# Recurrence, router and two feed-forward stages on one core: a written-out order with longer transfers and spare time for loads, and a first block inverted in two halves of 64 rows

## The chip, the cores and the metric

One NeuronCore of a Trainium2 chip. The time is device microseconds (us) of one execution. Engines: PE (TensorE; PEld its weight loads), DVE (VectorE), ACT (ScalarE), POOL (GpSimd), SP (SyncE, which issues nearly all DMAs). A run of the kernel before took 1150.17 us (median of 3).

## What is computed

```python
for t in range(S):                                # S = 768, 4 x 8 heads of 40
    y[:, :, t] = einsum('bhd,bhde->bhe', rt, state)
    Sa = einsum('bhde,bhe->bhd', state, at)
    state = state * wt - einsum('bhd,bhe->bhde', Sa, bt) + einsum('bhd,bhe->bhde', vt, kt)
# y as x[3072, 320] -> one of 8 experts each (argmax, softmax weight)
h = maximum(einsum('ecd,edf->ecf', disp, w1), 0); y = einsum('ecf,efd->ecd', h, w2)
# out = gate * y -> a dense pair of layers
h = x @ w_in; out = maximum(0.01 * h, h) @ w_out
```

## The kernel before

**The recurrence** (`attention`) does the 768 times in chunks of 32. A block `i` (6 of them) is four chunks for each of two groups of eight chunks; in the code a pair `n = 2i + hf` (hf 0 or 1), and within it four column groups `g`, which the loads and `prep` take two at a time (`h = 0` for g 0 and 1, `h = 1` for g 2 and 3). A **step** `s` is one (block, g, hf), `s = 8i + 2g + hf`: 48 steps, and step `s + 2` needs the state of step `s`.

For each block, ahead of its steps:
- `load` (L349 on, issued through `dma`, L343): decay `w`, keys `KB`, `AE`, from DRAM to SBUF, by SP;
- `prep` (L371 to L381): scans and products on DVE, some of them on POOL;
- `gram` (L397 on): 8 matmuls (L409; the profile counts each twice), a copy to `mab` by ACT, the store `Md<-mab`, and four masked copies into `AE` on DVE (L424);
- `inverse` (L438 on): `Mu<-Md` brings the block's 128 small triangular matrices back, one to a partition; POOL makes the start value `Tt` (L441, L442), DVE does 28 dependent operations (L450, L452), ACT or DVE copies the corner `Ta`, and SP stores `Td<-Tt` and `Tad<-Ta`;
- `back` (L456 on): `TB<-Td` (for each half `gp`) and four `Rt<-Tad` load them in the layout of the matmuls;
- `fix` (L465 on): matmuls L476 and L485 finish the inverse, for each `hf` and half `gp`.

Steps with g 0 and 1 use the half `gp` 0, the others `gp` 1. A step is `kbt` (L512), then `chain`: X (L542), u (L553, which is the first to need `fix`), state (L570, scaled into `MV` by DVE L574); then `output`: L590, L603, masks on DVE (L611), `py` (L622). After the four g of a pair the router (`Router.add`, L824 to L870) chooses experts and scatters the rows to DRAM. Then come the experts (L981, L1046) and the dense pair (L981, L1186), which the change does not touch.

**The order** is worked out while the program is built. `Sched.op` records each operation with its planned duration, what it reads and writes, and a due time; `Sched.run` places them one by one on V, A, P, T, S (DVE, ACT, POOL, PE, SP) by `level`, a due time less what still follows. `START` and `STEP` give the steps their due times, `DPREP`, `DINV`, `DFIX`, `DTURN`, `DOUT` those of the work around them, `RV0`, `ZR0` the earliest planned times of some DMAs. A transfer is planned as `nb / 360e3` us on one bus and seen .95 us after. Where the plan shows PE idle for over 0.24 us, `emit` puts filler matmuls ahead of the late operation (L724, `py<-one`, bf16 128 x 128, no use made of them) so that PE is not idle there. The engines then run in that order, each one in order, and wait on semaphores.

Of the kernel before, what the change touches and what calls it, by code (L numbers as in the profile page):

```python
# [10 lines left out]
ALU = mybir.AluOpType  # L11
# [15 lines left out]
class Sched:  # L27
# [7 lines left out]
    def __init__(self, eng):  # L35
        self.eng = dict(zip('VAPTS', eng))
        self.ops = []
        self.due = 1e9
        self.since = 0.
        self.slack = 0.  # L40
        self.w, self.r = {}, {}

    def op(self, on, dur, fn, r=(), w=(), ring=None, done=0., grp=None, xfer=0., banks=(), sel=False, act=None):
# [17 lines left out]
        self.ops.append(dict(on=on, fn=fn, deps=deps, ring=ring, done=done, grp=grp, users=0, ps=None, xfer=xfer, banks=list(banks), due=self.due, since=self.since, slack=self.slack, sel=sel, act=act))  # L61
        return i
# [20 lines left out]
    def run(self):  # L83
        ops = self.ops
        n = len(ops)
        succ = [[] for _ in ops]
        for i, o in enumerate(ops):
            for d in o['deps']:
                succ[d].append(i)
        lag = lambda o, e: self.AFTER[e] + o['done'] + (o['xfer'] + 1.5 if o['xfer'] else 0.)  # L90
        level = [0.] * n
        for i in range(n - 1, -1, -1):
            o = ops[i]
            e, d = min(o['on'].items(), key=lambda x: x[1])
            level[i] = d + max([level[j] + lag(o, e) for j in succ[i]] + [-o['due']])
        left = [len(o['deps']) for o in ops]
# [23 lines left out]
        while placed < n:  # L120
# [153 lines left out]
def attention(ctx, tc, I, R, eng):  # L274
# [62 lines left out]
    def masks(E):  # L337
# [4 lines left out]
        P.iota(maskZ.bitcast(I32)[:, D:D + 1], [[0, 1]], base=NT, channel_multiplier=0)  # L342
    def dma(o, i, nb, r, w, on='S'):  # L343
        op(on, .48 if on == 'S' else .06, lambda E: E.dma_start(o, i), r, w, xfer=max(.18, nb / 360e3))  # L344

# [3 lines left out]
    def load(n, h):  # L349
        i, hf = divmod(n, 2)  # L350
        a = n % 4
        late = ['Mu'] if n in (2, 3) else []
        dma(ws[hf][:, h, 0:528], I['wT'][hf, i, :, 528 * h:528 * h + 528], 270336, late if LATEW else (), [('w', hf, h)])
        dma(KBs[a][:, 2 * h:2 * h + 2].rearrange("x g p a t -> x (g p a t)"), I['kbT'][hf, i, :, 1024 * h:1024 * h + 1024], 1 << 19, late, [('KB', a, h)])
        src = I['aT'][hf, i].rearrange("x (j g c) -> x j g c", j=2, g=4)[:, :, 2 * h:2 * h + 2]
        zero = [('AEs', a, j, g, par) for j in range(2) for g in (2 * h, 2 * h + 1) for par in range(2)]
        if i:
            dma(AEs[a][:, :, 2 * h:2 * h + 2].rearrange("x j g p t -> x j (g p t)"), src.rearrange("x j g c -> x j (g c)"), 1 << 19, late, [('AEo', a, j, h) for j in range(2)] + zero)
# [78 lines left out]

    def inverse(i):  # L438

        dma(Mu, Mds[i % 2].rearrange("c u t s -> (c u) t s"), 1 << 19, [('Md', i % 2, c, par) for c in range(8) for par in range(2)], ['Mu'])  # L440
        op('P', 1.47, lambda E: (E.affine_select(Tt, Mu, [[-1, 32], [1, 32]], ALU.is_gt, 0.0, base=0, channel_multiplier=0),  # L441
                                 E.memset(Ttf[:, 0:1024:33], -1.0)), ['Mu'], ['Tt'])  # L442
        for k in range(1, 15):
            m = 15 - k
            if i:
                when(8 * i - 8 + DINV[0] + (DINV[1] - DINV[0]) * k / 14)
            tv = tmp[:, 0:2 * k * m].rearrange("u (x a b) -> u x a b", x=2, b=m)
            tt = Tb[:, :, 0:k, k + 1:16]
# [3 lines left out]
            op('V', d, lambda E, tv=tv, tt=tt: E.tensor_tensor(tt, tt, tv, ALU.subtract), ['tmp'], ['Tt'])  # L452
        op(ev(256, 'AV'), 0, lambda E: copy(E, Ta, Tt[:, 0:16, 0:16].rearrange("u a b -> u b a")), ['Tt'], ['Ta'])
        dma(Tds[i % 2].rearrange("u q s t -> (u q) s t"), Tt, 1 << 19, ['Tt'], [('Td', i % 2)], QI)
        dma(Tads[i % 2].rearrange("u q s t -> (u q) s t"), Ta, 1 << 17, ['Ta'], [('Tad', i % 2)], QI)

    def back(i):

        for gp in range(2):
            dma(TB4s[i % 2][:, gp].rearrange("s h u t -> s (h u) t"), Tds[i % 2][16 * gp:16 * gp + 16].rearrange("u q s t -> (q s) u t"), 262144,  # L460
                [('Td', i % 2)], [('TB', 4 * (i % 2) + 2 * gp + h) for h in range(2)], QI)
# [120 lines left out]
    def output(s):  # L582
# [41 lines left out]
        if g == 3:  # L624
            xk = []
            for bb in range(2):
# [3 lines left out]
                while u < 8 * bb + 8:  # L630
# [47 lines left out]
    for m, t in enumerate(NIs):  # L678
        for j in range(2):
            r = RHO[j]  # L680
            op(ev(320), 0, lambda E, t=t, r=r, j=j: copy(E, t[r:r + 64, j, :, :], ident[r:r + 64, r:r + 40].unsqueeze(1).broadcast_to([64, 8, 40])), (), [('NI', m, j, par) for par in range(2)])
    when(0)
    inverse(0)
    back(0)
    for x in range(4):
        when(2 * (x // 2) + x % 2)
        fix(0, x % 2, x // 2)
    Q.slack = 0.
    for i in range(6):
        if i < 5:  # L690
            for h in range(2):
                for n in (2 * i + 2, 2 * i + 3):
                    when(8 * i + DPREP[2 * h + n % 2])
                    load(n, h)
                    prep(n, h)
# [5 lines left out]
            for x in range(4):  # L701
                when(8 * i + DFIX + .5 + x // 2 * 1.5)
                fix(i + 1, x % 2, x // 2)
            when(8 * i + DTURN)
            turn(2 * i + 2)
            turn(2 * i + 3)
        for c in range(8):
# [8 lines left out]
            if i == 0 and c < 4:  # L716
# [710 lines left out]
```

## Time and profile before

| | us (or a count) |
|---|---|
| runs | 1150.17 (1149.91 to 1153.44), 3 runs |
| profiled execution: its time, its span | 1148.05, 1146.3 |
| step 0 (L553) to the last `py` of step 47 | 85.15 to about 543 |
| experts and dense pair, from 543 on | 603.3 |
| busy in the span | PE 1009.7, DVE 735.6, ACT 552.8, POOL 378.5 |
| PE's matmuls and weight loads; packets of the instruction queue q8 | 15,918 and 15,918; 127 |

The page gives totals; the kernel has stages, so a stretch is read at a time. Busy of PE is the union of its matmuls; "issue" as a releaser is time in which PE waited for nothing that the profile shows. A row of a timeline is start, duration, engine, line, operation, tiles, shapes and count.

### The profile page before, as it was taken

The page shows a single profiled execution, that of the slowest core. Times are in us where ns is not written, and L with a number is a line of the kernel's source. Part 1 is how long each engine was busy: PE and PEld are TensorE (multiplying, and loading weights), DVE is VectorE, ACT ScalarE, POOL GpSimd, SP SyncE. Part 2 cuts the span into 40 slices and gives each one's busy share as a digit, 9 for nine tenths or more (in the row PEclk, how much of TensorE's full clock was granted, in tenths as well). Part 3 has the DMA queues.
Part 4 walks back from the last instruction along what each step waited for, and adds up shares of the span by engine and source line. Part 5 has one row for each costly group of instructions (what it writes and reads, how often), then busy time and mean ns, then how long its engine had stood idle before and what let it go on. Part 6 is the DMA issues. An engine that isn't in the chain of part 4 may idle for free.

```text
span 1146.3 us, 37065 instructions
## 1 busy us (share of the span) xinstructions
PE 1009.7 (88%) x15918; PEld 906.1 (79%) x15918; DVE 735.6 (64%) x1571; ACT 552.8 (48%) x1264; POOL 378.5 (33%) x318
## 2 busy tenths in 40 slices
PE   4677777888878879989589999999999999999997
PEld 4665667777767767778588888999989999999997
DVE  7984676976967856344577787786764444444453
ACT  4114554856746747667434434434533333333343
POOL 8232112222223221010155565662849191010100
PEclk9876888998989988889799999999999999999999
DMA  7659463653734723330565666753311010000000
GB/s 201 202 135 250 100 164 90 178 150 110 194 98 146 172 64 98 72 98 12 165 224 175 199 197 199 217 170 107 99 32 51 18 30 18 7 18 7 23 13 14
DMA packets 146123, 129.44 MB, mean 113 GB/s; under 512 B 102176, under 2 KB 110624, under 8 KB 145952
## 3 DMA queue, kind: packets, MB, share of 16 engines
q1 hardware_dynamic: 143648, 119.11, 37.7%
q0 software_dynamic: 2304, 7.89, 1.9%
q8 instruction: 127, 2.08, 0.8%
q14 instruction: 44, 0.36, 0.1%
HBM read 102.13 MB, written 24.85 MB: 111 GB/s over the span
## 4 chain that ended last, share of the span: by engine, by line
PE 56%; DVE 14%; issue 13%; ACT 6%; DMA 5%; POOL 3%; SPq 3%; POOLq 0%; DVEq 0%; ACTq 0%
PE ph L981 17%; PE py L622 4%; PE oy L1188 3%; PE oy L1187 3%; PE oy L1186 3%; PE ch L570 2%; PE tr L590 2%; SPq L344 2%; PE tr L409 2%; ACT Z L292 2%; PE tr L512 2%; DVE tmp L450 2%; ACT NI L292 2%; PE y L1046 2%; PE tr L485 2%
## 5 line engine op out<-in xcount | busy, mean ns | idle before, releaser
L981 PE MATMUL ph<-xt,wq 128*128 128x512 f32 (+2 forms) x1408 | 311.5, 364 | 5.0 <-DVE xt L1022 5.0
L981 PEld LDWEIGHTS ph<-xt,wq 128*128 128x128 f32 x1408 | 248.0, 189 | 35.5 <-DVE xt L1022 6.5
L1166 DVE TENSOR_TENSOR gf<-gf,ph 128x512 f32<-128x512 f32 (+1 forms) x112 | 68.4, 610 | 98.8 <-ACT gf L1165 98.4
L1170 DVE TENSOR_TENSOR gl<-gf,gh 128x512 fp32r<-128x512 f32 (+1 forms) x112 | 76.7, 684 | 70.1 <-ACT gh L1169 70.1
L1165 ACT ACTIVATE gf<-ph 128x512 f32<-128x512 f32 (+1 forms) x112 | 60.0, 536 | 109.5 <-PE ph L981 109.0
L292 ACT COPY Z<-tr 40x512 f32<-40x512 f32 x192 | 98.3, 540 | 22.9 <-PE tr L590 21.2
L1169 ACT CAST gh<-gf 128x512 fp32r<-128x512 f32 (+1 forms) x112 | 62.7, 559 | 96.3 <-DVE gf L1166 96.3
L381 POOL TENSOR_TENSOR KB<-KB,w 128x1024 f32<-128x1024 f32 x21 | 47.2, 2245 | 159.4 <-PE py L622 34.4
L1196 POOL DMA_INDIRECT out_dram<-ob,gid x24 | 23.9, 995 | 218.5 <-ACT ob L1195 213.3
L1032 ACT ACTIVATE gh<-ph 128x448 fp32r<-128x448 f32 x64 | 34.9, 546 | 120.3 <-PE ph L981 120.3
L1188 PE MATMUL oy<-wo,gl 128*128 128x320 f32 x288 | 89.2, 310 | 0.1
L1187 PE MATMUL oy<-wo,gh 128*128 128x320 f32 x288 | 88.9, 309 | 0.0
L1186 PE MATMUL oy<-wo,gh 128*128 128x320 f32 x288 | 88.8, 308 | 0.0
L622 PE MATMUL py<-Z,RE 128*32 128x40 f32 x1536 | 73.7, 212 | 6.1 <-DVE RE L611 4.6
L611 DVE TENSOR_TENSOR RE<-tr,maskP 64x128 f32<-64x128 f32 x192 | 55.1, 287 | 34.3 <-PE tr L603 30.4
L622 PEld LDWEIGHTS py<-Z,RE 128*32 128x32 f32 x1536 | 65.8, 120 | 13.6 <-DVE RE L611 7.5
L1046 PE MATMUL y<-gh,wo 128*128 128x448 f32 x192 | 73.1, 381 | 3.0 <-DVE Y L1053 2.8
L574 DVE TENSOR_TENSOR MV<-ch,WC 40x320 f32<-40x320 f32 x92 | 44.9, 488 | 45.3 <-PE ch L570 43.7
L870 POOL DMA_INDIRECT xs<-xb,rii x24 | 25.6, 1068 | 142.0 <-DVE rii L860 95.2
L1049 PE MATMUL y<-gl,wo 128*128 128x448 f32 x192 | 70.9, 369 | 0.0
L292 ACT COPY NI<-tr 64x160 f32<-64x160 f32 x192 | 55.1, 287 | 23.3 <-PE tr L512 20.0
L590 PE MATMUL tr<-ident,MV 128*104 128x128 f32 x384 | 60.2, 290 | 5.1 <-ACT NI L292 4.1
(173 smaller groups left out, 2206.2 us busy)
## 6 DMA issues: line engine op xcount, KB each, us to landing
KB<-in_kbT_dram SPq DMA_DIRECT2D x24, 512.0 KB, 6.0
RE<-in_rT_dram SPq DMA_DIRECT2D x48, 256.0 KB, 4.3
AE<-in_aT_dram SPq DMA_DIRECT2D x20, 512.0 KB, 6.3
raw<-in_wo_dram SPq DMA_DIRECT2D x16, 640.0 KB, 5.2
raw<-in_wqa_dram SPq DMA_DIRECT2D x16, 512.0 KB, 4.1
w<-in_wT_dram SPq DMA_DIRECT2D x24, 264.0 KB, 4.6
xs<-maskZ SPq DMA_DIRECT2D x8, 563.5 KB, 5.5
win<-xs SPq DMA_DIRECT2D x8, 563.5 KB, 10.0
```

The costliest lines, as they stand in the source:

```text
L292: (E.copy if E is A else E.tensor_copy)(o, i)
L590: E.transpose(c['t'][0:104, q, :], MV[:, 4 * h + q], ident)
L622: E.matmul(py[32 * g:32 * g + 32, b, col:col + 40], RE[:, j, p, :], Z[:, p, ZC[j]:ZC[j] + 40], start=True, stop=True)
L981: T.matmul(ph, l, r, start=k == 0, stop=k == 7)
L1046: T.matmul(y[c], hi, gh, start=m == 0, stop=False)
L1049: T.matmul(y[c], hi, gl, start=False, stop=m == 7)
L1166: V.tensor_tensor(gf, gf, ph, ALU.max)
L1169: A.copy(gh, gf)
L1170: V.tensor_tensor(gl, gf, gh.bitcast(F32), ALU.subtract)
L1186: T.matmul(o, gh[:, sl], w[:, 0:320], start=m == 0, stop=False)
L1187: T.matmul(o, gh[:, sl], w[:, 320:640], start=False, stop=False)
L1188: T.matmul(o, gl[:, sl], w[:, 0:320], start=False, stop=m == 15)
```

## The change

The planner's transfers get longer: `nb / 230e3` us instead of `nb / 360e3`, seen 2.0 us after instead of .95. What needs a load is planned `SPARE` 5.11 + `LATE` 0.737 us after that (for the first reader; writers of a load's buffer add `SPARE` in `level`); operations of `fix` and of the router get .296 us, those of `output` .065 us more. The first block's inverse is recorded for `h` 0 and `h` 1 apart: `inverse(0, (h,))` works on 64 partitions, `back` and `fix` on one half, each behind that half's grams. Due times and earliest times have other values. The arithmetic is the same.

```diff
-        lag = lambda o, e: self.AFTER[e] + o['done'] + (o['xfer'] + 1.5 if o['xfer'] else 0.)
+        lag = lambda o, e: self.AFTER[e] + o['done'] + (o['xfer'] + 2.2 if o['xfer'] else 0.)
...
-            level[i] = d + max([level[j] + lag(o, e) for j in succ[i]] + [-o['due']])
+            level[i] = d + max([level[j] + lag(o, e) + ops[j]['spare'] for j in succ[i]] + [-o['due']])
...
-                seen = bus + .95
+                seen = bus + 2.
...
-                at[j] = max(at[j], seen)
+                at[j] = max(at[j], seen + ops[j]['spare'] + (self.LATE if o['free'] else 0.))
...
+    SPARE, LATE = 5.11, 0.737
-    SLACK, PATIENCE, ALPHA = 0.075, 30.677, 0.105
+    SLACK, PATIENCE, ALPHA = 0.075, 61.165, 0.105
...
-SLACK0, LD0, LDS, PR0, PRS, LATEW, RV0, ZR0, ZRS, GR = 0.268, 0.0, 3.0, 15.245, 0, 0, 40.584, 52.618, 7.65, 1
+SLACK0, LD0, LDS, PR0, PRS, LATEW, RV0, ZR0, ZRS, GR = 0.353, 0.0, 3.0, 14.965, 0.69, 0, 59.595, 76.525, 7.65, 1
...
-START, STEP = 66.553, 7.916
-DPREP, DINV, DOUT, DTURN, DFIX = (-1.52, -1.13, -0.18, 1.52), (2.13, 2.32), 1.968, 0.886, 6.599
+IN0, IN1, LD1 = -11.529, 31.742, 28.586
+LEAD, SPO, SPF = 0.74, 0.065, 0.296
+START, STEP = 42.156, 7.328
+DPREP, DINV, DOUT, DTURN, DFIX = (-2.42, -2.48, -0.18, 1.93), (2.35, 3.65), 1.966, 0.961, 7.992
...
-        op(on, .48 if on == 'S' else .06, lambda E: E.dma_start(o, i), r, w, xfer=max(.18, nb / 360e3))
+        op(on, .48 if on == 'S' else .06, lambda E: E.dma_start(o, i), r, w, xfer=max(.18, nb / 230e3), free=free)
...
-    def inverse(i):
+    def inverse(i, parts=(0, 1)):
...
+        o, n = 64 * parts[0], 64 * len(parts)
+        H, C = slice(o, o + n), range(4 * parts[0], 4 * parts[-1] + 4)
...
+        dma(Mu[H], Mds[i % 2][C[0]:C[-1] + 1].rearrange("c u t s -> (c u) t s"), 4096 * n, [('Md', i % 2, c, par) for c in C for par in range(2)], kM)
...
             for g in (2 * h, 2 * h + 1):
                 gram(n, g)
+        Q.due = IN0 + IN1 * h
+        inverse(0, (h,))
+        back(0, (h,))
+        for hf in range(2):
+            fix(0, hf, h)
...
-    when(0)
-    inverse(0)
-    back(0)
-    for x in range(4):
-        when(2 * (x // 2) + x % 2)
-        fix(0, x % 2, x // 2)
```

Line numbers of the changed kernel are higher: 344 became 349, 409 414, 424 429, 441 451, 450 460, 452 462, 476 487, 485 496, 553 564, 570 581, 724 743.

How it moves the instructions, at three places. **SP, from the first block's `Mu<-Md` on**, before:

```order
L344 DMA Mu<-Md_182 128x1024
L344 DMA KB_134<-in_kbT_dram 128x1024
L344 DMA AE_130<-in_aT_dram 128x2x512
L344 DMA KB_135<-in_kbT_dram 128x1024
L344 DMA AE_131<-in_aT_dram 128x2x512
```

and the changed kernel, from the second half's `Mu<-Md`:

```order
L349 DMA Mu<-Md_182 64x1024
L349 DMA Td_184<-Tt 64x1024
L349 DMA Tad_186<-Ta 64x256
L349 DMA TB_145<-Td_184 128x16x32
L349 DMA Rt<-Tad_186 16x16x16 x4
L349 DMA KB_135<-in_kbT_dram 128x1024
L349 DMA KB_134<-in_kbT_dram 128x1024
L349 DMA AE_131<-in_aT_dram 128x2x512
L349 DMA AE_130<-in_aT_dram 128x2x512
L349 DMA KB_134<-in_kbT_dram 128x1024
L349 DMA Td_184<-Tt 64x1024
```

The eight loads of block 1 (tiles 130, 131, 134, 135) stood between `Mu` and `Td`; now they stand behind the first half's stores and loads, and three of the eight behind the second half's stores.

**DVE, where the first block's inverse begins**, before:

```order
L424 TENSOR_TENSOR AE_129<-ch,maskP 32x4x32 x4
L371 SCALAR_TENSOR_TENSOR W<-w_126,d_178 128x528
L375 SCALAR_TENSOR_TENSOR w_126<-w_126,d_178 128x528
L372 COPY WC_155<-W 128x16
L373 RECIPROCAL rC_157<-WC_155 128x16
L374 TENSOR_TENSOR Q_166<-W,rC_157 128x2x8x32
L371 SCALAR_TENSOR_TENSOR W<-w_127,d_178 128x528
L450 TENSOR_TENSOR tmp<-Mu,Tt 128x28
```

and the changed kernel:

```order
L429 TENSOR_TENSOR AE_129<-ch,maskP 32x4x32 x4
L429 TENSOR_TENSOR AE_128<-tr,maskP 32x4x32 x4
L429 TENSOR_TENSOR AE_128<-ch,maskP 32x4x32 x4
L460 TENSOR_TENSOR tmp<-Mu,Tt 64x28
L462 TENSOR_TENSOR Tt<-Tt,tmp 64x2x14
L460 TENSOR_TENSOR tmp<-Mu,Tt 64x52
```

The six operations for block 1 and two of the eight groups of masks are no longer ahead of it, and its 28 operations follow each other with nothing between; the second half's 28 come eight instructions after.

**PE, around step 0** (L553 before, L564 now), before:

```order
L553 MATMUL ch<-X_163,TB_145 32x40 x16
L391 MATMUL tr<-ident,Q_167 128x128 x4
L485 MATMUL tr<-TB_145,Wm_174 32x16 x32
L570 MATMUL ch<-MV_117,NI_143 40x40 x16
L409 MATMUL tr<-AE_131,KB_135 64x64 x16
L553 MATMUL ch<-X_164,TB_145 32x40 x16
```

and the changed kernel:

```order
L564 MATMUL ch<-X_163,TB_145 32x40 x16
L553 MATMUL ch<-MV_118,AE_129 32x40 x16
L523 MATMUL tr<-ident,KB_133 128x128 x4
L581 MATMUL ch<-MV_117,NI_143 40x40 x16
L414 MATMUL tr<-AE_131,KB_135 64x64 x16
L414 MATMUL tr<-AE_130,KB_134 64x64 x8
L564 MATMUL ch<-X_164,TB_145 32x40 x16
```

Of block 1's eight grams (8 matmuls each) six stood ahead of step 0 and two ahead of step 1; now none, three ahead of step 1, and all eight ahead of step 2. Fillers: 715 in all before, 1,065 now; 445 of them stood ahead of step 0, now 325.

## Rows read from the trace of the kernel before

**Rows 1.** Stretches: length, busy (count) of PE, PEld, DVE, ACT, POOL, clock, DMA.
```profile
85.15:170.56 85.41, 62.75 (x1877) 53.38 (x1869) 52.37 (x126) 41.76 (x118) 13.16 (x8) 0.78 0.69 175
170.56:250.23 79.67, 66.55 (x2071) 58.24 (x2069) 63.00 (x175) 50.86 (x143) 24.26 (x19) 0.90 0.56 146
```
**Rows 2.** What PE waited for, 85 to 543: sum, times, longest.
```profile
PE tr L485 <- issue: 11.4, 8, 2.3
...
PE py L622 <- DVE RE L611: 4.6, 8, 1.1
...
PE py L724 <- issue: 0.3, 1, 0.3
```
**Rows 3.** PE's order in time, around one pause.
```profile
113.97 0.43 PE L553 MATMUL ch<-X,TB 32*32 32x40 f32 x27
119.98 0.34 PE L553 MATMUL ch<-X,TB 32*32 32x40 f32 x3 [5.57 <-issue]
```
**Rows 4.** DMA, 85 to 543: instruction queue (packets, MB), then KB each and us to landing.
```profile
q8 instruction: 94, 1.54, 1.4%
...
Mu<-Md SPq DMA_DIRECT2D x5, 512.0 KB, 4.8
Td<-Tt SPq DMA_DIRECT2D x5, 512.0 KB, 3.2
TB<-Td SPq DMA_DIRECT2D x10, 256.0 KB, 4.4
Md<-mab SPq DMA_DIRECT2D x70, 32.0 KB, 3.2
```
**Rows 5.** DVE in order of time.
```profile
41.99 1.18 DVE L424 TENSOR_TENSOR AE<-ch,maskP 32x128 f32<-32x128 f32 x4
...
49.04 0.15 DVE L450 TENSOR_TENSOR tmp<-Mu,Tt 128x28 f32<-128x28 f32 x1
...
67.10 0.21 DVE L452 TENSOR_TENSOR Tt<-Tt,tmp 128x28 f32<-128x28 f32 x1
...
94.95 1.18 DVE L424 TENSOR_TENSOR AE<-tr,maskP 32x128 f32<-32x128 f32 x4
```
**Rows 6.** SP and POOL in order of time.
```profile
23.83 2.32 SPq L344 DMA_DIRECT2D Md<-mab  x4
...
42.53 0.43 SPq L344 DMA_DIRECT2D KB<-in_kbT_dram  x1
...
46.46 1.56 POOL L441 TENSOR_SCALAR_AFFINE_SELECT Tt<-Mu 128x1024 f32<-128x1024 f32 x1 [13.35 <-DMA Mu<-Md]
```
**Rows 7.** A group of DVE: total busy, mean ns of one, idle before.
```profile
L452 DVE TENSOR_TENSOR Tt<-Tt,tmp 128x28 f32<-128x28 f32 (+6 forms) x84 | 21.3, 254 | 2.0
```
**Rows 8.** PE in order of time, up to step 8.
```profile
44.78 6.25 PE L724 MATMUL py<-one 128*128 128x128 bf16 x109
...
66.69 1.98 PE L409 MATMUL tr<-AE,KB 128*64 128x64 f32 x32 [3.95 <-DVE tmp L450]
...
75.10 1.06 PE L391 MATMUL tr<-ident,Q 128*128 128x128 f32 x8 [2.19 <-DVE Q L374]
...
81.92 0.68 PE L476 MATMUL tr<-Rt,TB 16*32 16x16 f32 x58 [0.18 <-DMA Rt<-Tad]
...
85.15 0.58 PE L553 MATMUL ch<-X,TB 32*32 32x40 f32 x19
...
99.73 0.47 PE L553 MATMUL ch<-X,TB 32*32 32x40 f32 x30
...
106.88 1.30 PE L570 MATMUL ch<-MV,NI 128*40 128x40 f32 x32
...
130.58 0.81 PE L570 MATMUL ch<-MV,NI 128*40 128x40 f32 x32
...
170.56 0.76 PE L553 MATMUL ch<-X,TB 32*32 32x40 f32 x32
```

More of the change, by code (lines that the diff above doesn't have):

```diff
@@ L40, in __init__, with op @@
         self.slack = 0.
+        self.spare = 0.
         self.w, self.r = {}, {}
-    def op(self, on, dur, fn, r=(), w=(), ring=None, done=0., grp=None, xfer=0., banks=(), sel=False, act=None):
+    def op(self, on, dur, fn, r=(), w=(), ring=None, done=0., grp=None, xfer=0., banks=(), sel=False, act=None, free=False):
         i = len(self.ops)
@@ L60, in op @@
         on = on if isinstance(on, dict) else {on: dur}
-        self.ops.append(dict(on=on, fn=fn, deps=deps, ring=ring, done=done, grp=grp, users=0, ps=None, xfer=xfer, banks=list(banks), due=self.due, since=self.since, slack=self.slack, sel=sel, act=act))
+        self.ops.append(dict(on=on, fn=fn, deps=deps, ring=ring, done=done, grp=grp, users=0, ps=None, xfer=xfer, banks=list(banks), due=self.due, since=self.since, slack=self.slack, sel=sel, act=act, free=free, spare=self.spare if on.keys() != {'S'} else self.SPARE if xfer and free else 0.))
         return i
@@ L357, in load @@
         if i:
-            dma(AEs[a][:, :, 2 * h:2 * h + 2].rearrange("x j g p t -> x j (g p t)"), src.rearrange("x j g c -> x j (g c)"), 1 << 19, late, [('AEo', a, j, h) for j in range(2)] + zero)
+            dma(AEs[a][:, :, 2 * h:2 * h + 2].rearrange("x j g p t -> x j (g p t)"), src.rearrange("x j g c -> x j (g c)"), 1 << 19, late, [('AEo', a, j, h) for j in range(2)] + zero, free=True)
         else:
@@ L436, in when @@
         Q.due = START + STEP * s
-    def inverse(i):
-        dma(Mu, Mds[i % 2].rearrange("c u t s -> (c u) t s"), 1 << 19, [('Md', i % 2, c, par) for c in range(8) for par in range(2)], ['Mu'])
-        op('P', 1.47, lambda E: (E.affine_select(Tt, Mu, [[-1, 32], [1, 32]], ALU.is_gt, 0.0, base=0, channel_multiplier=0),
-                                 E.memset(Ttf[:, 0:1024:33], -1.0)), ['Mu'], ['Tt'])
+    def inverse(i, parts=(0, 1)):
+        o, n = 64 * parts[0], 64 * len(parts)
+        H, C = slice(o, o + n), range(4 * parts[0], 4 * parts[-1] + 4)
+        kM, kT, kt = [[(x, h) for h in parts] for x in ('Mu', 'Tt', 'tmp')]
+        U = slice(o // 4, (o + n) // 4)
+        dma(Mu[H], Mds[i % 2][C[0]:C[-1] + 1].rearrange("c u t s -> (c u) t s"), 4096 * n, [('Md', i % 2, c, par) for c in C for par in range(2)], kM)
+        op('P', 1.47, lambda E: (E.affine_select(Tt[H], Mu[H], [[-1, 32], [1, 32]], ALU.is_gt, 0.0, base=0, channel_multiplier=0),
+                                 E.memset(Ttf[H, 0:1024:33], -1.0)), kM, kT)
         for k in range(1, 15):
@@ L452, in inverse @@
[L452 to L461, printed above, removed]
+            op('V', d, lambda E, tv=tv, k=k, m=m: E.tensor_tensor(tv, Mb[H, :, k:k + 1, k + 1:16].broadcast_to([n, 2, k, m]), Tb[H, :, 0:k, k:k + 1].broadcast_to([n, 2, k, m]), ALU.mult),
+               kM + kT, kt)
@@ new lines, in inverse @@
+            op('V', d, lambda E, tv=tv, tt=tt: E.tensor_tensor(tt, tt, tv, ALU.subtract), kt, kT)
+        op(ev(256, 'AV'), 0, lambda E: copy(E, Ta[H], Tt[H, 0:16, 0:16].rearrange("u a b -> u b a")), kT, [('Ta', h) for h in parts])
+        dma(Tds[i % 2][U].rearrange("u q s t -> (u q) s t"), Tt[H], 4096 * n, kT, [('Td', i % 2, h) for h in parts], QI)
+        dma(Tads[i % 2][U].rearrange("u q s t -> (u q) s t"), Ta[H], 1024 * n, [('Ta', h) for h in parts], [('Tad', i % 2, h) for h in parts], QI)
@@ L462, in back @@
+    def back(i, parts=(0, 1)):
+        for gp in parts:
+            dma(TB4s[i % 2][:, gp].rearrange("s h u t -> s (h u) t"), Tds[i % 2][16 * gp:16 * gp + 16].rearrange("u q s t -> (q s) u t"), 400000,
+                [('Td', i % 2, gp)], [('TB', 4 * (i % 2) + 2 * gp + h) for h in range(2)], QI)
+        g, e = parts[0], parts[-1] + 1
         for q in range(4):
-            dma(R4[32 * q:32 * q + 16].rearrange("s m u t -> s (m u) t"), Tads[i % 2][:, q].rearrange("u s t -> s u t"), 80000, [('Tad', i % 2)], [('Rt', m, q) for m in range(4)], QI)
+            dma(R4[32 * q:32 * q + 16, 2 * g:2 * e].rearrange("s m u t -> s (m u) t"), Tads[i % 2][16 * g:16 * e, q].rearrange("u s t -> s u t"), 80000, [('Tad', i % 2, h) for h in parts], [('Rt', m, q) for m in range(2 * g, 2 * e)], QI)
@@ L636, in output @@
                     u += m
+            Q.spare = SPF
             R.add(Q, psum, copy, ev, hf, i, xk)
+            Q.spare = SPO
     Q.slack = SLACK0
@@ L692, in attention @@
                 for n in (2 * i + 2, 2 * i + 3):
+                    when(8 * i + DPREP[2 * h + n % 2] - LEAD)
+                    Q.since = 0. if i else LD1
+                    load(n, h)
+                    Q.since = 0.
                     when(8 * i + DPREP[2 * h + n % 2])
-                    load(n, h)
                     prep(n, h)
@@ L721, in attention @@
             when(s + DOUT)
+            Q.spare = SPO
             output(s)
+            Q.spare = 0.
     Q.run()
```

20 lines of the change are left out of this document (10 added, 10 removed).

## The prediction

> **What bounds the kernel now.** The stretches come first. From step 8 on a block takes some 80 us, of which PE is busy 66.55 of 79.67; the first block's stretch takes 85.41 with 62.75 busy and a granted clock of 0.78, against 0.90 after [rows 1]. So PE is near its limit once the recurrence runs, and in the first block it has both the lower clock and more idle time. Next, what PE waited for from 85 us to 543: the ten groups "issue" sum to 57.9 us, and the largest named wait is only 4.6 [rows 2]. The timeline shows what such a pause is: 27 of 32 matmuls of one group run, then nothing for 5.57 us, then the rest [rows 3]. The same stretch has 94 packets on the instruction queue, 1.54 MB [rows 4]: a pause inside one group fits instructions that come late. What the change retimes, the waits for loads, is therefore not what PE loses most by after step 8. The start is another matter. The reader should see in the timelines that PE fills 6.25 us with 109 fillers at 44.78 [rows 8], while DVE does the inverse from 49.04 to 67.31 [rows 5] and SP then stores and reloads it; `fix` runs at 81.92 and step 0 at 85.15 [rows 8]. This chain bounds the first 85 us.
>
> **The change, part by part.**
>
> *Step 0 comes sooner.* The first half needs only the first four grams. Before, their four stores were issued until 26.15 [rows 6]; landing takes 3.2, then `Mu` 4.8 for 512 KB [rows 4] (taken whole: half as many bytes may be faster), with some 1 us of issue between: 35.1. POOL needs 1.56 [rows 6]: 37. DVE could begin the inverse at 49.04 less the 5.9 us between the masks' end (43.17) and there, less two of eight mask groups, 2.4 (two rows like 1.18): 40.7 [rows 5]. I take 39, between the two. 28 operations of 0.254 [rows 7] and small gaps, none interleaved, take 7.5, to 46.5; before they took 18.3. Half as many partitions is taken as no shorter; the bounds are 4 and 7.5. `Td` 3.2 and `TB` 4.4 [rows 4], with about 1.5 of issue: 55.6. From the last `fix` start to step 0 took 3.2 [rows 8]: step 0 at 58.5 to 59, **26.5 us sooner**. If each hop takes its longer bound and DVE the 40.7, it is 22; if half the bytes and rows are faster, 30.
> The rows give a landing of 3.2 us for as little as 32 KB and 4.8 for 512 KB [rows 4]. The Trainium skill ("DMA: Bandwidth & Descriptors", Anatomy of one DMA) fits a fixed 2.0 us and bytes over 436 GB/s, for a DMA issued another way. By it three hops of 256 KB would take 2.6 each (an estimate from that page), and step 0 would come some 4 us earlier still; the rows stand against it, and nothing below uses it.
>
> *Work moves behind step 0.* Six of block 1's grams stood ahead of step 0 and stand after it: three rows of 32 matmuls like 1.98, 5.6 in all, and two L391 groups, one row of 1.06 [rows 8]. **+6.7 us** on PE.
>
> *Fillers.* 350 more in all, but 120 fewer ahead of step 0, where PE is idle anyway; so 470 more after it. One takes 6.25 / 109 = 0.057 us [rows 8]: 26.8 us of PE. They stand where the plan sees a wait, and the plan now puts 5.11 + 0.74 us behind every load's landing. Where PE would have waited anyway, a filler costs nothing; where the load has long landed, its whole time. Bounds 0 and 26.8. The named waits are so small [rows 2] that most of the padding behind loads can't be real, but in the first block, now begun with less other work in hand, the order has the state's own chain to wait for, which is. I take half: **+13.4**.
>
> *Clock.* PE at 0.78 is at 1.2 GHz some 0.44 of the time. The same 32 matmuls take 1.30 there and 0.81 at 2.4 [rows 8]. If fillers lift the first block halfway to the 0.90 of the next [rows 1], 0.12 less of 62.75 us runs slow, and (1 - 0.81 / 1.30) of that is won: **-2.8**. Bounds 0 and -10.4 (none and all of the 0.44).
>
> *Costs beside other work.* 28 more DVE operations (7.1 us), 1.7 more on POOL, seven more DMA issues on SP (about 0.45 each). DVE has 33 us idle in the first block's stretch [rows 1], and the second half's inverse runs while step 0 waits for its transfers: nothing, and at most 7.1 if block 1's preparation, which DVE does next, is what PE waits for. The eight loads of block 1 were issued from 42.53 [rows 6]; now they are behind the first half's `Rt`, about 51.5. That is 9 us later, and block 1's grams on PE are behind them. I cost it at nothing as long as fillers and steps 0 and 1 cover it; the second rival is what happens if not.
> The span's 31,836 matmuls and weight loads came in 127 packets (the table), 251 each, so 700 more are 2.8 packets. The pauses come to 57.9 / 94 = 0.62 us a packet [rows 2, 4]: some 1.7 us, which I leave within the rounding. The Trainium skill ("Runtime: NRT & Kernel Launch", Instruction fetch mechanics) says that the fetch of the next block of instructions is mostly hidden; by it the sum would lose this term, and the 5.57 us pause speaks against it.
>
> Sum: -26.5 + 6.7 + 13.4 - 2.8 = **-9.2 us** on the profiled execution's 1148.05: 1138.9. Experts and dense pair are the same instructions. The median of the runs is 2.1 above the profiled one; with it, 1141. I say **1140**.
>
> **The rivals.**
>
> *The whole start is kept*: nearly all new fillers stand in real waits and the clock rises. Then, with 1 us left of the fillers and the clock nearer its bound, -26.5 + 6.7 + 1 - 8 = -27: 1122. For it: the first block's low clock. Against it: small named waits.
>
> *The start's gain ends at step 2.* All eight grams of block 1 now stand ahead of step 2's u on PE. They need the loads, 9 us later than before, and DVE's preparation. Before, its last masks ended at 96.1 and step 2 ran at 99.73 [rows 5, 8]. From 43.17 to 96.1 DVE spent 18.3 on the inverse, so 34.7 on the rest; begun again behind the second half's inverse, at about 57, it ends at 92. Then step 2 gains 6 or 7 only, and of the fillers some 370 come after it: half of them, +10.6, and the clock, -2.8, leave +1: 1149 to 1151. No change. It decides if PE stands before block 1's grams with its fillers done.
>
> *Slower: the fillers are simply work.* PE has little slack after step 8, and a filler that covers no wait delays every step behind it. With none covered and the clock as before: -26.5 + 6.7 + 26.8 = +7: 1157. It decides if fewer than (26.8 + 6.7 - 26.5) / 26.8, about a quarter, of the new fillers stand in waits. For it: the 240 fillers from step 8 on become 430, where PE waited least. Against: the plan of before left the waits of the first block without fillers.
>
> *The change does nothing*, because the halves are serialised again: the second half's `Mu` stands ahead of the first half's `Td` on SP, so the first half's stores wait for the second half's grams. Their masks ended at 43.17 before [rows 5], ahead of the 46.5 at which `Td` is ready, so I give it no chance of its own.
>
> **How the numbers follow.** Forecast 0.50, of which a little ends near no change; whole start kept 0.14; ends at step 2 0.16; slower 0.20. Less than 0.3%, about 3.4 us, can't be told from no change. Faster: 0.46 + 0.14 = 0.60; same 0.04 + 0.14 = 0.18; slower 0.20 + 0.02 = 0.22. The likeliest case's own range is 1127 to 1149. The range for 8 in 10 takes in most of the two outer cases: 1119 to 1156, leaving out the half of the first below its 1122 and those of the slower that are worse than 1156 because loads come late too.
>
> **What would show it.** Step 0's u at 57 to 63 us and the first half's inverse begun near 39, in under 8 us: the start is right. Step 2's u at 99.73 less 7 or more, and step 8's below 165, would show it kept; step 2 at 92 to 98 and step 8 at 168 to 172, the second rival. Whether the fillers cover waits shows in the blocks from step 8 on: at 79.67 or less they do, at 82 or more they don't. A clock above 0.84 in the first block shows that term. I am wrong at the root if step 0 isn't at least 15 us sooner, or if blocks after step 8 lose or win more than 4 us each, which the views of before give no reason for.

## The result and the profile after

The changed kernel takes **1162.22 us** (median of 4 runs, 1161.25 to 1169.63), the kernel before beside it 1150.53 (1149.91 to 1153.44): ratio 1.0118, 95% interval 1.0078 to 1.0158. It is 1.2% slower; the forecast was 1140, and 1162 lies outside its range of 1119 to 1156. The profiled execution has a span of 1161.3 (before 1146.3).

Three stretches divide the difference: up to step 8's u, from there to the first matmul of the experts, and the rest. The first fence is the view by stretches of the kernel before (length, busy of PE with its matmuls, PEld and the other engines, granted clock, DMA), for the first two, then the same for the fillers alone (L724); the second fence is the changed kernel (fillers L743).

```profile
0.00:170.56 170.56, 115.44 (x2820) 102.34 (x2820) 126.28 (x269) 64.77 (x172) 56.51 (x80) 0.83 0.66 176
170.56:558.51 387.95, 322.78 (x9931) 280.66 (x9930) 255.68 (x787) 249.74 (x693) 83.62 (x77) 0.89 0.44 114
...
0.00:170.56 170.56, 32.68 (x475) 30.48 (x475) 0.83 0.66 176
170.56:558.51 387.95, 22.20 (x240) 16.33 (x240) 0.89 0.44 114
```

```profile
0.00:169.55 169.55, 126.53 (x3004) 113.99 (x3004) 136.07 (x306) 74.02 (x195) 57.86 (x84) 0.86 0.64 167
169.55:573.40 403.85, 337.69 (x10097) 292.93 (x10096) 255.42 (x769) 243.86 (x678) 86.81 (x77) 0.87 0.43 114
...
0.00:169.55 169.55, 44.60 (x635) 40.85 (x635) 0.86 0.64 167
169.55:573.40 403.85, 35.36 (x430) 27.56 (x430) 0.87 0.43 114
```

Taking the fillers from PE's busy time leaves its own work, and taking all of it from the length leaves idle time:

| us | before | after |
|---|---|---|
| up to step 8: length | 170.56 | 169.55 |
| own work / fillers / idle | 82.8 / 32.7 / 55.1 | 81.9 / 44.6 / 43.0 |
| step 8 to the experts: length | 387.95 | 403.85 |
| own work / fillers / idle | 300.6 / 22.2 / 65.2 | 302.3 / 35.4 / 66.2 |
| experts to the end of the span | 587.8 | 587.9 |

So the first part gained 1.0 us, the second lost 15.9, and the third didn't move. In the second, own work and idle time are within 2 us of before, and the fillers take 13.2 us more. In these two executions it looks as if the fillers were the whole loss; the experiments say otherwise.

Step 0 did come sooner. PE in order of time, for [rows 8]:

```profile
52.56 0.64 PE L487 MATMUL tr<-Rt,TB 16*32 16x16 f32 x6 [1.53 <-DMA Rt<-Tad]
...
57.95 1.56 PE L496 MATMUL tr<-TB,Wm 32*32 32x16 f32 x98 [2.62 <-ACT Wm L489]
...
62.19 0.76 PE L564 MATMUL ch<-X,TB 32*32 32x40 f32 x32
...
85.98 4.01 PE L743 MATMUL py<-one 128*128 128x128 bf16 x69
...
96.87 3.93 PE L414 MATMUL tr<-AE,KB 128*64 128x64 f32 x64
...
104.19 0.49 PE L564 MATMUL ch<-X,TB 32*32 32x40 f32 x32
```

Step 0's u is at 62.19 instead of 85.15, but step 2's at 104.19 instead of 99.73, behind the last of block 1's grams (64 matmuls at 96.87). DVE, for [rows 5]:

```profile
37.34 0.18 DVE L460 TENSOR_TENSOR tmp<-Mu,Tt 64x28 f32<-64x28 f32 x1
...
45.73 0.20 DVE L462 TENSOR_TENSOR Tt<-Tt,tmp 64x28 f32<-64x28 f32 x1
...
49.14 0.18 DVE L460 TENSOR_TENSOR tmp<-Mu,Tt 64x28 f32<-64x28 f32 x1
...
58.36 1.26 DVE L376 TENSOR_TENSOR_SCAN W<-w,d 128x528 f32<-128x528 f32 x1
59.65 2.41 DVE L380 TENSOR_TENSOR_SCAN w<-w,d 128x528 f32<-128x528 f32 x2
61.97 2.09 DVE L377 COPY WC<-W 128x16 f32<-128x16 f32 x1
...
98.04 4.85 DVE L429 TENSOR_TENSOR AE<-tr,maskP 32x128 f32<-32x128 f32 x16 [6.90 <-PE tr L414]
```

The first half's inverse runs from 37.34 to 45.93, the second's from 49.14, and from 58.36 on DVE prepares block 1. It shows no wait from 26.99 to 91.14 (60.58 us busy of 64.15); then it waits 6.90 for PE, which runs the second half's `fix` and fillers ahead of block 1's last grams. Block 1's last masks end at 102.9, before at 96.1.

The blocks, for [rows 1]: first before, from step 16 and 24, then the change, from step 0, 8, 16 and 24. Behind them PE's waits in the change from 85 to 556, for [rows 2]:

```profile
250.23:330.93 80.70, 67.78 (x2073) 58.98 (x2070) 60.40 (x174) 50.50 (x143) 19.70 (x17) 0.89 0.52 137
330.93:408.97 78.04, 64.47 (x2057) 55.95 (x2057) 61.27 (x176) 50.27 (x141) 21.95 (x18) 0.94 0.51 135
```

```profile
62.19:169.55 107.36, 88.38 (x2244) 78.68 (x2243) 80.71 (x180) 55.63 (x156) 25.91 (x15) 0.85 0.63 164
169.55:253.45 83.90, 67.74 (x2095) 58.28 (x2093) 63.75 (x167) 47.83 (x134) 22.46 (x18) 0.91 0.53 141
253.45:344.45 91.00, 78.92 (x2159) 68.73 (x2157) 67.86 (x189) 53.27 (x150) 23.88 (x18) 0.80 0.51 140
344.45:427.79 83.34, 68.41 (x2090) 59.45 (x2089) 58.41 (x174) 51.65 (x144) 21.60 (x18) 0.90 0.49 130
```

```profile
PE tr L496 <- issue: 19.8, 10, 3.7
PE tr L487 <- issue: 13.5, 13, 4.1
PE py L633 <- DVE RE L622: 9.5, 12, 3.1
```

The blocks from step 8, 16 and 24 are 4.2, 10.3 and 5.3 us longer; the block from step 32 is 4.5 shorter, and the last, up to the experts, 0.5 longer. A block isn't the same work in both: the plan moves operations from one to the next. The wait for RE is 9.5 where it was 4.6; the pauses ahead of `fix` (L487, L496) are longer, the others shorter, and all of "issue" is 41.4 instead of 57.9. No wait has grown by 15.9.

### The profile page after: what moved, and what is told of

Its sections match the earlier page's. It is cut to its first block, busy times and chain, and to the rows that moved or that the text cites. A ratio compares the mean times of both kernels' runs of the same rounds, so it can differ in the third digit from the quotient of the medians.

```text
span 1161.3 us, 37747 instructions
## 1 busy us (share of the span) xinstructions
PE 1035.9 (89%) x16268; PEld 930.3 (80%) x16268; DVE 746.0 (64%) x1591; ACT 555.8 (48%) x1271; POOL 381.8 (33%) x322
## 4 chain that ended last, share of the span: by engine, by line
PE 53%; DVE 16%; issue 16%; DMA 6%; ACT 4%; POOL 3%; SPq 1%; POOLq 0%; DVEq 0%; ACTq 0%
PE ph L1000 13%; PE py L633 5%; PE py L743 3%; PE tr L601 2%; PE ch L581 2%; PE oy L1207 2%; PE oy L1206 2%; PE oy L1205 2%; DVE tmp L460 2%; PE tr L414 2%; ACT Z L297 2%; PE tr L496 2%; PE tr L614 2%; DVE Tt L462 2%; PE tr L487 2%
## 5 line engine op out<-in xcount | busy, mean ns | idle before, releaser
L1189 DVE TENSOR_TENSOR gl<-gf,gh 128x512 fp32r<-128x512 f32 (+1 forms) x112 | 76.8, 686 | 70.1 <-ACT gh L1188 70.1
L297 ACT COPY Z<-tr 40x512 f32<-40x512 f32 (+1 forms) x192 | 98.4, 540 | 29.8 <-PE tr L601 28.1
L889 POOL DMA_INDIRECT xs<-xb,rii x24 | 29.3, 1219 | 174.8 <-DVE rii L879 168.9
L633 PEld LDWEIGHTS py<-Z,RE 128*32 128x32 f32 x1536 | 68.5, 124 | 18.8 <-DVE RE L622 12.7
L743 PE MATMUL py<-one 128*128 128x128 bf16 x1065 | 80.0, 231 | 3.8 <-DVE xb L645 2.3
L622 DVE TENSOR_TENSOR RE<-tr,maskP 64x128 f32<-64x128 f32 x192 | 55.1, 287 | 38.3 <-PE tr L614 31.0
L743 PEld LDWEIGHTS <-one 128*128 128x128 bf16 x1065 | 68.4, 104 | 8.4 <-issue 3.7
L585 DVE TENSOR_TENSOR MV<-ch,WC 40x320 f32<-40x320 f32 x92 | 44.9, 488 | 46.5 <-PE ch L581 41.5
L383 POOL TENSOR_TENSOR AE<-AE,Q 64x512 f32<-64x512 f32 x21 | 31.2, 1486 | 117.2 <-DMA AE<-in_aT_dram 39.9
```

The costliest lines, as they stand in the source:

```text
L297: (E.copy if E is A else E.tensor_copy)(o, i)
L633: E.matmul(py[32 * g:32 * g + 32, b, col:col + 40], RE[:, j, p, :], Z[:, p, ZC[j]:ZC[j] + 40], start=True, stop=True)
L1189: V.tensor_tensor(gl, gf, gh.bitcast(F32), ALU.subtract)
```

## The experiments

Ratios are to the kernel before in the same set of runs, with 95% intervals. The medians of before in the four sets were 1148.36 (e1 to e4), 1143.81 (e5 to e8), 1152.03 (e9 to e12) and 1146.38 (e13 to e15), so an expected total is to be read with a few us to either side, and the ratio decides. Times of single places come from one profiled execution each, and these scatter: behind step 8 the order of before took from 383.1 us (e13) to 398.3 (e9) in six of them, with 296.7 to 306.0 us of own work and 62.3 to 71.2 idle. The changed order took 399.4 to 407.8 in five. The diffs are shortened, some to a sketch of the edit. Theory A, at the beginning: the start's gain is given back to block 1's preparation by step 8, and the order behind step 8 loses some 16 us.

**One part of the change at a time.** e1 puts the halves into the kernel before, with its constants:

```diff
+        when(2 * h)
+        inverse(0, (h,)); back(0, (h,))
+        for hf in range(2):
+            when(2 * h + hf); fix(0, hf, h)
```

> The order, constants and transfer model of before, with only the first block's inverse, its transfers and its fix split in two halves of 64 rows, due at steps 0 and 2. Theory A (the start is won, but is given back to block 1's preparation by step 8, and what comes after step 8 loses some 16 us by the new order): step 0's u near 60 to 65, step 8's u at 166 to 171, the blocks behind it as before (79 to 81 us), total 1143 to 1151. Rival, the halves' gain is real and only the rest of the change spoils it: step 8's u at 150 to 160 and total 1127 to 1140. Rival, the halves themselves cost: total above 1154.

Measured: 1154.32, ratio 1.0074 (1.0042 to 1.0105). Step 0's u was at 87.5, not at 60: with these due times the first half's inverse ran mixed with block 1's preparation, from 44.4 to 68.0. So the first part of the expectation was wrong. By its total the third rival (above 1154) was met, but the run, which has 28 DVE operations and seven transfers more and another order, doesn't tell which of them costs the 0.7%. Its profiled execution was its fastest (1144.1), with 386.1 us behind step 8 as before, and so doesn't show where the loss stands.

e2 takes the halves out of the changed kernel:

```diff
-        Q.due = IN0 + IN1 * h
-        inverse(0, (h,))
...
+    Q.due = IN0
+    inverse(0)
+    back(0)
```

> The changed kernel with the first block inverted whole, as before the change; everything else of the change stays. Theory A: step 0's u back at 80 to 86, step 8's u at 168 to 175 all the same, and the blocks behind it as slow as in the change: total 1160 to 1168, so the halves bring nearly nothing. Rival, the halves do bring their 23 us and the rest of the change costs 35: total 1178 to 1186.

Measured: 1162.52, ratio 1.0153 (1.0093 to 1.0213). Its profiled execution was the longest of six (span 1174.1), with step 0's u at 109.6: later than the 80 to 86 expected, and 47 us later than in the change. Step 8's was at 187.5, not at 168 to 175: a start as late as this did reach step 8, 18 us later. The median is that of the change all the same, so the halves bring little to the total.

e4 sets the four spare times to 0:

```diff
-    SPARE, LATE = 5.11, 0.737
+    SPARE, LATE = 0.0, 0.0
-LEAD, SPO, SPF = 0.74, 0.065, 0.296
+LEAD, SPO, SPF = 0.74, 0.0, 0.0
```

> The changed kernel with all four spare times at zero (5.11 and 0.737 for loads, 0.065 and 0.296 us for operations); the longer transfers of the plan, the due times and the halves stay. If the spare times spoil the blocks: those from step 8 on fall back to at most 80 us each, step 8's u comes at 160 to 170, total 1140 to 1152. Rival, the new due times or the longer transfers do it: the blocks stay at 83 us and over, total 1158 to 1168.

Measured: 1157.50, ratio 1.0100 (1.0052 to 1.0148), step 0's u at 78.9, step 8's at 166.5. It can't be told from the change's 1.0118, so taking the spare times out doesn't win the loss back. As this is another new plan, it doesn't show either that they are harmless.

**Are the fillers work?** e3 keeps the changed order and drops 190 of the 430 fillers behind step 8; e8 drops all 310 between the u of steps 0 and 8.

```diff
+    for each operation behind u(8): fill = fill * 240 // 430      # e3
+    for each operation from u(0) to u(8): fill = 0                # e8
```

> The changed kernel's own order, instruction for instruction, but from step 8's u on only 240 of its 430 fillers, as many as before the change. Rival, fillers are simply work: 190 x 0.057 = 10.8 us less behind step 8, total 1149 to 1153. Theory A as far as it puts the loss on the order and not on the fillers: at most 3 us less, total 1159 to 1164, or more if the granted clock falls by the missing fillers.

> The changed kernel's order without the 310 fillers between the u of step 0 and that of step 8 (23.0 us of PE in the profile). If they cover waits that DVE and POOL set (block 1's preparation, on which DVE works without a gap until 91 us): step 8's u at 167 to 171 as before, and total 1158 to 1164, a lower granted clock in that stretch included. Rival, they are work: step 8's u near 150, total 1140 to 1148.

Measured: e3 1160.99, ratio 1.0131 (1.0081 to 1.0180). Its stretch behind step 8, all of PE and the fillers alone:

```profile
169.76:575.22 405.46, 332.23 (x9908) 285.33 (x9906) 257.76 (x769) 244.14 (x678) 85.08 (x77) 0.87 0.42 113
...
169.76:575.22 405.46, 23.57 (x240) 15.66 (x240) 0.87 0.42 113
```

The fillers take 11.8 us less, the idle time is 73.2 (7.1 more) and the own work 308.7 (6.3 more, for the same matmuls). The stretch is no shorter, nor is the median. How the 11.8 us divide between waits and slower matmuls one execution can't tell: 6 us is the scatter given above.

e8: 1161.92, ratio 1.0166 (1.0128 to 1.0203). Its first block, and step 8:

```profile
63.28:170.04 106.76, 74.94 (x1933) 63.22 (x1932) 79.48 (x180) 55.51 (x156) 24.84 (x15) 0.77 0.63 165
```

```profile
170.04 0.49 PE L564 MATMUL ch<-X,TB 32*32 32x40 f32 x32
```

23.0 us of fillers less, and step 8 is at 170.04 instead of 169.55. Own work is 74.94 us instead of 65.34, at a granted clock of 0.77 instead of 0.85. Step 2's u does come sooner, at 100.4 instead of 104.19, and step 8 gains nothing by it. The rival "they are work" falls in both stretches.

**Start or rest?** e5 and e6 plan both orders in one kernel and splice them at step 8's u.

```diff
+    Q1, Q2 = plan(new constants), plan(old constants)   # e6: the other way
+    emit Q1.order up to u(8), with what it has begun
+    emit the rest in Q2.order, with Q2's fillers
```

> Both orders are planned and spliced: the changed order up to and with step 8's u, and behind it every instruction in the order of before, with the fillers of before (236 behind step 8 instead of 430). Theory A (the start brings nothing, the loss is in the order behind step 8): step 8's u at 168 to 171 and the blocks behind it within 1 us of those of before on average, total 1146 to 1151. Rival, what the changed start leaves behind at step 8 (less work done ahead) is what makes the blocks longer: they stay 3 us or more longer, total 1156 to 1163.

> The splice the other way: the order of before up to and with step 8's u, the first block inverted whole, and behind it the changed order with its 430 or so fillers. Theory A: step 8's u at 170 to 171, and the blocks and the tail behind it as long as in the change: total 1160 to 1166. Rival, the loss comes with the changed start: total 1147 to 1153.

Measured: e5 1142.21, ratio 0.9988 (0.9964 to 1.0013), step 8's u at 167.87; e6 1166.71, ratio 1.0204 (1.0175 to 1.0232), step 8's at 170.19. Behind step 8, e5 and e6:

```profile
167.87:556.58 388.71, 318.05 (x9903) 275.49 (x9902) 254.88 (x770) 243.92 (x678) 81.80 (x77) 0.88 0.45 119
```

```profile
170.19:578.02 407.83, 340.57 (x10161) 295.90 (x10159) 259.25 (x786) 249.50 (x694) 86.07 (x77) 0.89 0.42 109
```

388.71 and 407.83 against 387.95 before and 403.85 in the change. The ratios say the same: the loss goes with the order behind step 8, and both rivals fall. e6 lies 0.9% above the change, which theory A doesn't explain.

The largest part of it stands in one block. From step 16 to step 24 the five executions with the changed order (the change, e3, e6, e8, e10) took 90.2 to 91.0 us, with 67.1 to 72.7 of own work; the six with the order of before (before, e5, e9, e13, e14, e15) took 78.6 to 83.7, with 61.9 to 64.2. In the change the block holds 2,072 matmuls of own work, before 2,020, so part of this is work moved in from its neighbours; why the rest is slower isn't shown.

**Is it the new rules, or any new order?** e7 and e11 move one due time of the kernel before by 0.4 and 0.8%, e12 one of the change by 0.4%.

```diff
-START, STEP = 66.553, 7.916
+START, STEP = 66.553, 7.95        # e7
-DFIX = 6.599
+DFIX = 6.65                      # e11
-START, STEP = 42.156, 7.328
+START, STEP = 42.156, 7.36        # e12
```

> The kernel before with one number of its due times moved by 0.4% (STEP 7.95 instead of 7.916) and nothing else: another order of the same work by the same rules. Theory A: the loss of the change comes from its rules (spare times, longer transfers, due times), so this one stays within 0.3% of before, 1145 to 1152. Rival D, any new order of this planner costs about 1%, because the order of before is a lucky one: 1154 to 1165.

> The kernel before with another due time moved by 0.8% (DFIX 6.65 instead of 6.599), nothing else. Theory D (the order of before is one good draw, and a new order by the same rules costs about 1%; the first such one took 0.87% more): 1152 to 1162. Rival, the first was bad luck and near orders are as good as before: within 0.3%, 1141 to 1150.

> The changed kernel with one due time moved by 0.4% (STEP 7.36 instead of 7.328). Theory D: another draw from the same spread as the re-plans of before, 1148 to 1168, not tied to the 1.2% of the change. Rival, the change's rules themselves (spare, longer transfers) make every order slower: 1158 to 1172, and the blocks from step 8 on at 82 us and over again.

Measured: e7 1152.42, ratio 1.0087 (1.0055 to 1.0118); e11 1169.97, ratio 1.0136 (1.0090 to 1.0182); e12 1170.14, ratio 1.0163 (1.0125 to 1.0200). By its time e7 lies between theory A (to 1152) and rival D (from 1154); its ratio, 0.9% where A allowed 0.3%, is for D, which the next run took up as a theory. e11 is slower than D's 1152 to 1162, e12 than its 1148 to 1168. So the sizes were missed, but an order made by the rules of before, from a due time moved by less than 1%, costs about as much as the whole change. In its profile e7 has 21.8 us of fillers behind step 8, as before, and takes 400.6 there. e12 lies in its rival's range, and its blocks from step 8, 16 and 24 pass 82 us: that the new rules cost something of their own isn't excluded.

**What holds step 8?** e9 splices at step 0's u instead: the new start, then everything in the order of before, without the fillers that stood ahead of step 0 there. e10 is the change without the 28 DVE operations of the second half's inverse.

```diff
-        if i == Q1.mark[8]:
+        if i == Q1.mark[0]:          # e9
+            skip = i == 0 and parts == (1,)   # e10: L460 and L462 issue nothing
```

> The changed order only up to and with step 0's u (first half inverted, step 0 near 62 us), then the second half's transfers, and everything else in the order of before, without the fillers that before had ahead of its step 0: 290 or so fillers less than the splice at step 8. If block 1's preparation on DVE sets step 8 whatever stands ahead of it: step 2's u at 98 to 105, step 8's at 166 to 172, total 1143 to 1151. Rival, the prediction's own view that step 0's time carries through when the order behind it doesn't put block 1's grams ahead: step 8's u at 145 to 158, total 1122 to 1136.

> The changed kernel without the 28 DVE operations of the first block's second half (that half of the inverse is left out; its transfers, its fix and every other instruction stay). If DVE's own work sets the start: block 1's preparation ends 7.5 us sooner on DVE, step 2's u comes at 95 to 98 and step 8's at 162 to 165, total 1152 to 1158. Rival, DVE isn't what holds step 8 (transfers, PE's order and the chain of block 1 are): step 2's u 2 to 5 us sooner and step 8's at 168 to 171, total 1159 to 1165.

Measured: e9 **1144.23, ratio 0.9934 (0.9906 to 0.9962)**, faster than both kernels; its profiled execution was its longest (1153.1). As the best of fifteen kernels it may owe part of this to the luck of its order. Step 8's u is at 162.82, between the two theories. What PE waited for between step 0 and step 8 there (sum, times, longest):

```profile
PE tr L405 <- DVE Q L388: 10.7, 2, 6.2
PE tr L423 <- POOL AE L392: 4.6, 1, 4.6
PE ch L573 <- issue: 4.0, 1, 4.0
```

L405 and L423 are the turns and grams of block 1: PE waits 15.3 us for its preparation on DVE and POOL. e10: 1158.66, ratio 1.0062 (1.0034 to 1.0089). Block 1's last masks and the u of steps 2 and 8:

```profile
93.34 4.85 DVE L429 TENSOR_TENSOR AE<-tr,maskP 32x128 f32<-32x128 f32 x16 [6.14 <-PE tr L414]
```

```profile
99.24 0.49 PE L565 MATMUL ch<-X,TB 32*32 32x40 f32 x32
...
166.19 0.80 PE L565 MATMUL ch<-X,TB 32*32 32x40 f32 x32
```

Step 2 is 5.0 us sooner, step 8 3.4: also between the two. DVE's work is part of what holds step 2. For step 8 the 3.4 us are little above the scatter: with the changed order up to there its u was at 167.87 (e5), 169.55 and 169.76 (e3).

Three more runs on the order of e9. e13 puts all that the u of steps 1 to 3 need ahead of block 1's preparation; e14 issues POOL's six multiplications for block 1 to DVE, in the same places; e15 does both.

```diff
+    need.add(Q1.mark[3])                                # e13, e15
+    if name in prep(2), prep(3): engine = DVE           # e14, e15
```

> As the splice at step 0 (changed order to step 0, then the order of before), but everything that the u of steps 1, 2 and 3 needs is put directly behind step 0, ahead of block 1's preparation and grams on every engine. Theory P (block 1's preparation, some 35 us of DVE and POOL from 58 us on, and the chain behind it set step 8, whatever PE does in between): step 3's u at 78 to 90 instead of 109, but step 8's still at 160 to 168, total within 0.4% of that splice, 1137 to 1150. Rival Q (PE's waiting ahead of block 1's grams is what is lost): step 8's u at 145 to 155 and total 1125 to 1136.

> As the splice at step 0, but block 1's multiplications that stood on POOL (L383 and L386 of the changed kernel for block 1) are issued to DVE, where they stand in the same place of the order. Theory P with the stretch seen in the trace (a DVE copy of 0.15 us takes 2.1 beside a POOL multiplication, some 10 us in all from 58 to 91 us): DVE's operations there keep their own times, the added ones take 0.69 and some 1.2 us, and block 1's last masks end within 4 us of 97, step 8's u within 4 us of 163, total 1138 to 1150. Rival: DVE is simply overloaded by some 7 us, step 8's u at 167 to 175, total 1148 to 1158.

> The two edits of the last two together. Theory P: whichever of the two shortens block 1's preparation moves step 8, and putting steps 1 to 3 ahead alone doesn't: total within 0.4% of the better of the two. Rival Q: at least 5 us below both.

Measured: e13 1150.72, ratio 1.0033 (0.9997 to 1.0069); e14 1145.91, ratio 0.9968 (0.9934 to 1.0002); e15 1149.62, ratio 1.0008 (0.9972 to 1.0044). PE in e13:

```profile
73.57 0.76 PE L573 MATMUL ch<-X,TB 32*32 32x40 f32 x32
...
80.82 1.98 PE L423 MATMUL tr<-AE,KB 128*64 128x64 f32 x32 [4.58 <-POOL AE L392]
...
88.99 1.94 PE L405 MATMUL tr<-ident,Q 128*128 128x128 f32 x8 [6.19 <-DVE Q L388]
```

Step 2's u is at 73.57, 26 us sooner than before, and step 8's at 168.49: later than in e9. PE's waits for block 1 are the same, only later. Step 3 wasn't moved as expected (104.9; its u stands behind these grams after all). Rival Q falls. Theory P's numbers were missed as well: step 8's by 0.5 us, and the total is 1% above e9's by the ratios, where it allowed 0.4%. In e14 step 8 is at 165.16 and block 1's last masks end at 95.1, within the ranges of theory P; e15 is 0.4% above e14, at the edge of its range. So PE's order between steps 0 and 2 doesn't bring step 8 forward. That block 1's preparation sets step 8 is not shown, and the end of the preparation alone doesn't. The end of block 1's inverse on DVE and its first `fix` on PE, before and in the change:

```profile
142.12 0.21 DVE L452 TENSOR_TENSOR Tt<-Tt,tmp 128x28 f32<-128x28 f32 x1
...
158.26 0.49 PE L476 MATMUL tr<-Rt,TB 16*32 16x16 f32 x4
```

```profile
135.43 0.18 DVE L462 TENSOR_TENSOR Tt<-Tt,tmp 128x28 f32<-128x28 f32 x1
...
158.56 0.73 PE L487 MATMUL tr<-Rt,TB 16*32 16x16 f32 x64
```

The change's last masks end 6.8 us later than those of before, its inverse ends 6.7 sooner, and `fix` begins at the same time: from inverse to `fix` it is 23.0 us instead of 15.9, and 13.9 in e9. From block 1's last masks to step 8's u it is 66.7 us in the change, 74.4 before, 65.8 in e9 and 70.1 in e14. The stores, the reloads, other transfers (the DMA share is 1.00 to 1.08 from 110 to 130 in the change) and PE's order stand in between. Which of these sets the end wasn't tried.

All runs together: five kernels have the order of before behind step 8 or step 0 (e5, e9, e13, e14, e15) and lie at 0.9934 to 1.0033; the change and ten kernels with another order lie at 1.0062 to 1.0204.

## Why the prediction was wrong, point by point

*Step 0 sooner by 26.5.* Right in kind: 23.0. The inverse was at 37.34 to 45.93 (39 to 46.5 in the text). What was mis-sized is the end: from the first `fix` matmul to step 0 it took 9.6 us, where the text took 3.2 from the last `fix` start (4.7 from the first, at 80.50), since both steps' `fix` stand in between, with a wait of 2.62 and a pause of 1.08.

*That this moves the end.* Here the sum failed: "This chain bounds the first 85 us" was read as if the whole program stood behind step 0. What stands behind it is step 8, and that came at 163 to 171 with step 0 anywhere from 62 to 88, in every profile but that of e2. The second rival had the place ("the start's gain ends at step 2") and step 8's time (169.55 in its 168 to 172), though not step 2's (104 where it said 92 to 98), and priced it as no change. Its own rows give step 2 a gain of 4.1 us (96.1 to 92), not the 6 or 7 that it takes, and so some 3 us more time.

*Costs beside other work, at nothing.* Right for block 1's loads, 9 us later, as DVE came to block 1 only at 58.36. Wrong for DVE: the 33 us of idle time in [rows 1] lie mostly behind block 1's preparation (25 of them after 96.13), and from 27 to 91 us DVE now has no wait. Without the 28 operations step 2 came 5.0 us sooner (e10).

*Work behind step 0, +6.7.* PE's own work ahead of step 0 fell from 22.0 to 16.6, 5.4 moved. As the sum over the start shows, it changes nothing at step 8.

*Fillers, half of 26.8.* Behind step 0 they take 58.4 us instead of 24.2, 34.2 more for 470: 0.073 each, where the long row of [rows 8] gave 0.057; many stand in short rows (4 take 0.61 us at 74.69). But e3 and e8 show that taking them away gains nothing. The lower bound, 0, was the one, and the slower rival ("the fillers are simply work", 1157) came nearest to the time by a mechanism that didn't happen.

*Clock, -2.8.* The first block's clock is 0.85, as said (0.84); in e8 it is 0.77 and step 8 stays. It is worth nothing there.

*What the sum left out.* It had no term for the order behind step 8, since "the views of before give no reason" for blocks to change. That is the step whose failure decided, and the prediction had named its sign: blocks that lose more than 4 us each. Its other sign, blocks of 82 us or more, it would have read as fillers that cover nothing, and e3 speaks against that. Between the two profiled spans (15.0 us apart) the stretch behind step 8 lost 15.9 and all the rest gained 0.9. A plan from new numbers is a new order of the same work, and its price showed in e7 and e11 to be about 1% without any change of rules. Why the order of before is that much better stays open: the largest part of the loss stands in the block from step 16, with more own work there, and no single wait carries it.

*A reading.* In [rows 3] two of the 32 matmuls run ahead of the 27 shown, so 29 had run at the pause; nothing in the sum hangs on it.

## What to carry to other kernels

When a change passes through a planner, compare it with the kernel planned again from numbers moved by half a percent, and splice old and new order at a point where the work is the same: this helps to tell the change from the luck of an order, the better the more such plans are run. Behind a step that comes sooner, look for the next one that other work holds, and price the gain there. An account of one trace (own work, fillers, idle) says where the time stands, not what would go if one of the three were cut.

## What the runs showed of the hardware

The preparation of block 1 stretches itself. The groups of DVE from 57 to 99 us in e9 (mean ns of one), where POOL works for 13.01 us, and in e14, where it does nothing:

```profile
L392 DVE TENSOR_TENSOR AE<-AE,Q 64x512 f32<-64x512 f32 x6 | 5.8, 963 | 0.2
...
L388 DVE TENSOR_TENSOR Q<-W,rC 128x512 f32<-128x512 f32 x3 | 3.8, 1264 | 0.1
L386 DVE COPY WC<-W 128x16 f32<-128x16 f32 x3 | 2.4, 803 | 0.0
```

```profile
L392 DVE TENSOR_TENSOR AE<-AE,Q 64x512 f32<-64x512 f32 x8 | 5.5, 686 | 0.2
...
L395 DVE TENSOR_TENSOR KB<-KB,w 128x1024 f32<-128x1024 f32 x4 | 4.8, 1203 | 0.0
L388 DVE TENSOR_TENSOR Q<-W,rC 128x512 f32<-128x512 f32 x3 | 2.1, 692 | 0.1
...
L386 DVE COPY WC<-W 128x16 f32<-128x16 f32 x3 | 0.5, 165 | 0.0
```

A copy of 165 ns takes 803 in the mean beside POOL (2.09 us in the fence of the change above), a product 1264 instead of 692. DVE took over six multiplications that cost POOL 13.01 us, and was busy 36.56 us of these 42 instead of 33.89. The Trainium skill ("SBUF — State Buffer", SBUF: two separate sides) describes a port pair as an exclusive lock that DVE, in some kinds of operation, or GpSimd holds for a whole instruction while the other waits; the copy's 803 ns beside POOL against 165 without agree with it. The masks, which read PSUM, keep their 284 ns in both.

PE's pauses of "issue" fell from 57.9 us [rows 2] to 41.4, with 94 packets on the instruction queue in both stretches (85 to 543 before, 85 to 556 in the change), and 33.3 of the 41.4 stand in the two groups of `fix` (L487, L496), matmuls of 16 columns. So a pause isn't a fixed price of a packet, as the prediction's 0.62 us took it.
